# Weight loads move from SyncE's DMA queue to ScalarE's, and a padding write moves behind the first loads

## The chip, the cores and the metric

One NeuronCore of a Trainium2 chip runs the whole program. The metric is device time in microseconds (us), from the run's own time measurement; the profiler adds one profiled execution, whose span is counted from its first to its last instruction. The engines are named as in the profile: PE (matrix multiply), PEld (its weight loads), DVE (VectorE), ACT (ScalarE), POOL (GpSimd) and SP (SyncE). SP computes nothing here; it issues transfers. ACT and POOL can issue transfers too, as instructions in their own streams. A "q" behind an engine's name in the profile (SPq, ACTq) means its sequencer, which issues transfers and waits on semaphores, in order.

## The reference

```python
# 1. a gated linear scan over time, per batch and channel (4 x 5056 tokens, 256 channels)
sig = 1.0 / (1.0 + np.exp(-f_logit))
f = lower_bound + (1.0 - lower_bound) * sig
i = 1.0 - f
for t in range(S):
    h = f[:, t] * h + i[:, t] * x[:, t]
    y[:, t] = h
# 2. a mixture of 8 experts over the 20224 tokens of y, one expert per token
e_idx = np.argmax(y @ w_gate, axis=1)
gate_w = softmax(y @ w_gate)[token, e_idx]
eom = 1.0 / (1.0 + np.exp(-(y @ w_output_gate)))
for e in range(8):
    h = np.maximum(y[e_idx == e] @ w1[e], 0.0)          # 256 -> 1024
    out[e_idx == e] = gate_w * eom[:, e] * (h @ w2[e])  # 1024 -> 256
```

## The kernel before

The tokens are taken in 40 chunks of 512. For a chunk, `load_chunk` (lines 241 to 252) brings f and x, 512 KB each; below they are called f0 and x0 for chunk 0, f1 and x1 for chunk 1, and so on. `chunk` (line 254) then runs Tanh on ACT (line 265), a product on DVE (269), an affine step on ACT (274), the scan on DVE (280), a Square with a sum on ACT (287), a split of the result into a high and a low float16 part (310 on ACT, 314 on DVE), a transpose of these by DMA from SP (307), the gate logits and the choice of an expert (329 to 430), and last the scatter of the token rows from POOL into a scratch array in DRAM, sorted by expert (433). `scr` is that array; its last 128 rows are padding rows for tiles that have nothing to do, written once from the tile `padt` (lines 208 to 212).

An expert's tile of tokens is fetched from `scr` with two SP transfers, a transposing gather and its small metadata (`gather`, lines 624 to 638), goes through two matrix products, a scaling on ACT and a scatter from POOL into the output (754). There are two kinds of tiles. The "first" tiles (`first1`, `first2`, lines 712 to 741; 16 of them, 128 tokens each) run early, while the weights are still being prepared. The main tiles (`gemm1`, `gemm2`, lines 666 to 709) run in the long stage that begins at about 187 us.

The weights come as float32 and are turned into scaled float16 high and low parts. There are 16 halves (w1 and w2 of eight experts). `prep_load(j)` (lines 562 to 568) brings half j in two 512 KB pieces into the tile pool `wp`, which has 8 buffers, so four halves are there at a time. `prep_gram` and `prep_sum` (570, 590) find the scale on PE, `prep_hi` (612) writes the high part on ACT (line 614), `prep_lo` (616) the low part on DVE (line 619). Once the low part is written, the two buffers are free for half j + 4.

The order: lines 877 to 882 load chunks 0, 1 and 2 and halves 0 to 3, in the source order chunk 0, chunk 1, half 0, chunk 2, halves 1 to 3. The loop from line 884 on goes through the halves. At step j it issues `prep_load` for half j + 3 (line 886), runs pieces of the chunks and of the scaling, and feeds first tiles in between. `ordered` (lines 915 to 923) fixes what may be rearranged: up to the end of this early stage the instructions on DVE, ACT, PE and POOL are free, and the scheduler orders them by when they can run; SP's transfers keep the order of the source throughout, and behind the early stage everything does.

Of the kernel before, what the change touches and what calls it, by code (L numbers as in the profile page):

```python
# [45 lines left out]
def raw(ins):  # L46
    return getattr(ins, "ins", ins)
# [3 lines left out]
def tile_scan_moe(  # L51
# [10 lines left out]
    nc = tc.nc  # L62
    P = 128
# [10 lines left out]
    FREE = E * R  # L74
# [3 lines left out]
    WH = WE // 2  # L78
    QH = WH // 2
# [4 lines left out]
    def sure(tokens):  # L84
# [10 lines left out]
    scr = dp.tile([E * R + P, RW], I16, name="scr")  # L95
# [8 lines left out]
        out=tri, in_=ones, compare_op=ALU.is_gt, fill=0.0, base=0, pattern=[[1, P]], channel_multiplier=-1  # L104
# [63 lines left out]
    def alone(g):  # L168
# [12 lines left out]
        out=gsq, in0=wgf, scalar=1.0, in1=wgf, op0=ALU.mult, op1=ALU.mult, accum_out=gss  # L181
# [9 lines left out]
        out=wgs[:, :, 1, :], in0=wgc, scalar=gsc, in1=wgs[:, :, 0, :], op0=ALU.mult, op1=ALU.subtract  # L191
# [3 lines left out]
    fresh = []  # L195

    def apart(ins, group, keep=()):
        tc.declare_no_dep(raw(ins), group=group, keep=[raw(k) for k in keep], reason="rows apart")
        tc.add_to_no_dep_group(group, raw(ins))
# [8 lines left out]
    padt = cp.tile([P, RW], I16, name="padt")  # L208
    nc.gpsimd.memset(padt, 0)
    nc.gpsimd.iota(padt[:, CM + 2 : CM + 4].bitcast(I32), pattern=[[0, 1]], base=N, channel_multiplier=0)  # L210
    fresh.append(nc.sync.dma_start(out=scr[FREE : FREE + P, :], in_=padt))
    apart(fresh[0], "scr")
    row2 = [cp.tile([P, NB, RW], I16, name=f"rows{i}") for i in range(2)]

    top1 = w1f[:, (E - 1) * 2 * WH : E * 2 * WH]
# [346 lines left out]
    def prep_load(j):  # L562
        ws = []
        for i in range(2):
            w = wp.tile([P, QH], F32, tag="w", name="w")
            nc.sync.dma_start(out=w, in_=wT[j // 2][:, j % 2 * WH + i * QH : j % 2 * WH + (i + 1) * QH])
            ws.append(w)
        half[j] = dict(w=ws)

    def prep_gram(j):  # L570
        H = half[j]
        H["pg"] = pg = pp.tile([P, P], F32, tag="h", name="pg", bufs=4)
        nq = QH // P
        for i in range(2):
            rr = H["w"][i].bitcast(BF16).rearrange("p (c two) -> p c two", two=2)[:, :, 1]
            for q in range(nq):
                part = rr[:, q * P : (q + 1) * P]
                nc.tensor.matmul(out=pg, lhsT=part, rhs=part, start=(i + q == 0), stop=(i == 1 and q == nq - 1))

    def prep_norm(j):  # L580
        H = half[j]
        l2 = sp.tile([P, 1], BF16, tag="l2", name="l2")
        yield BIG
        jk = sp.tile([P, P], F16, tag="jk", name="jk", bufs=1)
        nc.vector.scalar_tensor_tensor(
            out=jk, in0=H["pg"], scalar=1.0, in1=ident, op0=ALU.mult, op1=ALU.mult, accum_out=l2
        )
        H["l2"] = l2

    def prep_sum(j):  # L590
        half[j]["pb"] = pb = pp.tile([P, 1], F32, tag="rw", name="pb")
        nc.tensor.matmul(out=pb, lhsT=ones, rhs=half[j]["l2"], start=True, stop=True)

    def prep_scale(j):
        H = half[j]
        H["sc"], H["iv"] = yield from pow2(H["pb"], TW, "w")
        if j % 2:
            e = j // 2
            yield SMALL
            nc.vector.scalar_tensor_tensor(  # L600
                out=cinv[:, e : e + 1], in0=half[j - 1]["iv"], scalar=0.125, in1=H["iv"], op0=ALU.mult, op1=ALU.mult
            )
# [9 lines left out]
    def prep_hi(j, z):  # L612
        h, r = parts(j, 0, z)
        nc.scalar.activation(h, r, AF.Copy, scale=half[j]["sc"])

    def prep_lo(j, z):
        (h, r), (l, _) = parts(j, 0, z), parts(j, 1, z)
        yield BIG
        nc.vector.scalar_tensor_tensor(out=l, in0=r, scalar=half[j]["sc"], in1=h, op0=ALU.mult, op1=ALU.subtract)
# [190 lines left out]
    def step(k, tasks, need=PLAN):  # L810
        prog["left"] += k
        if prog["left"] < 1.0:
            together(tasks)
        while prog["left"] >= 1.0:
            prog["left"] -= 1.0
            pump(tasks, need)
            tasks = []
# [17 lines left out]
    def early(j):  # L835

        if not line or line[0]["half"] == 1 and len(line) == 1:
            for r in range(len(firsts)):
                e = turns[r]
                if e < min(E, (j + 1) // 2) and (r == 0 or e < turns[r - 1]):  # L840
                    T = gather(f"f{r * E + e}", firsts[r][e], e)
                    T["half"] = 0
                    line.append(T)
                    turns[r] += 1
                    break
        tasks, wait, ready, late = [], list(pend), list(over), list(mid)
        pend.clear()
        over.clear()
        mid.clear()
        for T, h in wait:  # L850
            tasks.append(first_low(T, h))
            if h == 0:
                tasks.append(factors(T))
        go = line and line[0]["ev"] < j // 2

        def rest():
            for T in ready:
                evacuate(T)
                put(T)
            if go:  # L860
                T, h = line[0], line[0]["half"]
                T["half"] += 1
                if h == 1:
                    line.pop(0)
                first1(T, h)
                pend.append((T, h))
            for T, h in late:
                first2(T, h)
                if h == 1:
                    over.append(T)  # L870
            mid.extend(wait)

        return tasks, rest
# [3 lines left out]
    for n in range(min(EARLY[0], NCH)):  # L877
        load_chunk(n)
        if n:
            prep_load(n - 1)  # L880
    for n in range(min(EARLY[0], NCH) - 1, deep):
        prep_load(n)
    for j in range(-2, nh):
        tasks = []
        if 1 <= j < nh + 1 - deep:
            prep_load(j - 1 + deep)
        if 0 <= j + 1 < nh:
            tasks.append(prep_scale(j + 1))
        for z in range(2):
            if 0 <= j:  # L890
                tasks.append(prep_lo(j, z))
            mine, rest = early(j)
            tasks += mine
            step((PUMPS if j >= TURN else PUMPS0 if j >= 0 else FILL) / 2, tasks, LEAD)
            if 0 <= j + 1 < nh:
                prep_hi(j + 1, z)
            rest()
            tasks = []
            if j + 2 < nh:
                if z == 0:  # L900
                    prep_gram(j + 2)
                    tasks.append(prep_norm(j + 2))
                else:
                    prep_sum(j + 2)
# [110 lines left out]
```

## Time and profile before

| what | value |
|---|---|
| median of 3 runs | 1020.92 us (1020.44 to 1021.68) |
| the profiled execution's own time | 1019.5 us |
| its span | 1017.8 us |
| busy PE / PEld / DVE / ACT / POOL | 917.6 / 822.5 / 886.5 / 511.8 / 378.2 us |
| weight loads (line 566) | 32 of 512 KB, all on SP |
| chunk loads (lines 250, 251) | 80, all on SP |
| other transfers of ACT's queue | 2 (lines 122 and 123) |

How to read it: a line of the timeline gives the start, the time, the engine, the line of the kernel, the operation with its output and input, and how many of them the row merges; in brackets stands how long the engine was idle before, and what ended the idle time. A line of the waits gives who waited, for whom, the total in us, how often, and the longest. For a transfer, the row of SPq or ACTq is the issue, not the transfer itself; when it lands is seen at the instruction that waited for it.

### The profile page before, as it was taken

What the parts mean: (1) busy time and instruction counts of PE and PEld (TensorE: products, weight loads), DVE (VectorE), ACT (ScalarE), POOL (GpSimd) and SP (SyncE); (2) the same over time, 40 slices, a digit from 0 to 9 for tenths busy, and PEclk for the clock granted to TensorE, in tenths of its full rate; (3) what the DMA queues carried; (4) which work ended last, traced back from release to release, by engine and by line L of the source; (5) the groups of instructions that cost most, each with busy time, mean ns of one, the idle gap of its engine ahead of it and who ended that gap; (6) DMA issues with size and microseconds to landing.
All of it is one profiled execution on the core that took longest, in us unless ns stands there. A gap on an engine that the chain in (4) does not pass through costs nothing. (4 is left out here: it accounts for less than half of the span.)

```text
span 1017.8 us, 27499 instructions
## 1 busy us (share of the span) xinstructions
PE 917.6 (90%) x9775; PEld 822.5 (81%) x9775; DVE 886.5 (87%) x2803; ACT 511.8 (50%) x1075; POOL 378.2 (37%) x378
## 2 busy tenths in 40 slices
PE   2267998899999999999999999999999999999993
PEld 2156987788888888888888888888888888899993
DVE  7889897899999999999999999999999998758771
ACT  5667684554554555545545455455455543333331
POOL 1532334334344443433444434344444344221121
PEclk9999999999999999999999999999999999999997
DMA  8899976755655556456566555565565644321120
GB/s 311 200 305 271 254 179 147 163 154 137 139 136 151 145 136 163 135 136 142 132 141 156 157 147 133 136 139 132 142 154 135 151 91 97 97 54 43 43 55 16
DMA packets 238546, 146.34 MB, mean 144 GB/s; under 512 B 202557, under 2 KB 204223, under 8 KB 238400
## 3 DMA queue, kind: packets, MB, share of 16 engines
q1 hardware_dynamic: 222752, 101.74, 43.5%
q0 software_dynamic: 15360, 42.74, 13.3%
q8 instruction: 80, 1.31, 0.6%
q14 instruction: 66, 0.54, 0.2%
q10 hardware_dynamic: 288, 0.02, 0.0%
HBM read 58.38 MB, written 44.49 MB: 101 GB/s over the span
## 5 line engine op out<-in xcount | busy, mean ns | idle before, releaser
L675 PE MATMUL ph<-xq,w 128*128 128x256 f16 (+1 forms) x1312 | 331.0, 261 | 3.2 <-DMA xq<-scr 2.7
L677 PE MATMUL ph<-xq,w 128*128 128x256 f16 (+1 forms) x1312 | 331.6, 261 | 0.0
L676 PE MATMUL ph<-xq,w 128*128 128x256 f16 (+1 forms) x1312 | 331.3, 261 | 0.0
L706 PE MATMUL py<-w,hh 128*128 128x256 f16 x1168 | 318.0, 272 | 10.4 <-DVE w L663 5.5
L708 PE MATMUL py<-w,hl 128*128 128x256 f16 x1168 | 318.3, 273 | 0.0
L707 PE MATMUL py<-w,hh 128*128 128x256 f16 x1168 | 318.2, 272 | 0.0
L754 POOL DMA_INDIRECT out_dram<-yo,mt x146 | 165.9, 1137 | 298.4 <-ACT yo L750 270.5
L433 POOL DMA_INDIRECT scr<-rows,dst x154 | 178.9, 1162 | 225.3 <-issue 212.5
L680 ACT ACTIVATE hh<-ph 128x512 f16<-128x512 f32 (+1 forms) x328 | 178.7, 545 | 156.9 <-PE ph L677 154.9
L688 DVE SCALAR_TENSOR_TENSOR hl<-ph,hh 128x512 f16<-128x512 f32 (+1 forms) x328 | 204.8, 625 | 10.4 <-ACT hh L680 8.6
L675 PEld LDWEIGHTS <-w 128*128 128x128 f16 x1312 | 128.0, 98 | 16.5 <-DVE xt L269 3.0
L677 PEld LDWEIGHTS <-w 128*128 128x128 f16 x1312 | 128.1, 98 | 12.1
L657 DVE COPY w<-w1s 128x2048 f16 x164 | 114.9, 701 | 26.2 <-PE ph L677 24.7
L676 PEld LDWEIGHTS <-w 128*128 128x128 f16 x1312 | 127.9, 97 | 9.7
L707 PEld LDWEIGHTS <-hh 128*128 128x128 f16 x1168 | 113.9, 98 | 23.2 <-issue 12.7
L708 PEld LDWEIGHTS <-hl 128*128 128x128 f16 x1168 | 113.9, 98 | 13.5
L706 PEld LDWEIGHTS <-hh 128*128 128x128 f16 x1168 | 113.9, 98 | 11.2
L663 DVE COPY w<-w2s 128x2048 f16 x164 | 111.9, 682 | 0.5 <-PE py L708 0.3
L274 ACT ACTIVATE ft<-ft,fb,fa 128x512 f32<-128x512 f32 (+1 forms) x76 | 60.6, 807 | 97.9 <-DVE xt L269 90.1
L310 ACT ACTIVATE ft<-xt,sa 128x512 f16<-128x512 f32 (+1 forms) x76 | 50.2, 708 | 104.9 <-DVE li L299 100.7
L280 DVE TENSOR_TENSOR_SCAN xt<-ft,xt 128x512 f32<-128x512 f32 (+4 forms) x78 | 90.9, 1173 | 0.0
L750 ACT ACTIVATE yo<-py,fac 128x256 f32<-128x256 f32 x146 | 61.5, 465 | 26.4 <-PE py L708 22.8
(172 smaller groups left out, 1355.0 us busy)
## 6 DMA issues: line engine op xcount, KB each, us to landing
ft<-in_fT_dram SPq DMA_DIRECT2D x37, 512.0 KB
xt<-in_xT_dram SPq DMA_DIRECT2D x37, 512.0 KB
w<-in_wT_dram SPq DMA_DIRECT2D x32, 512.0 KB
scr<-rows,dst POOLq DMA_INDIRECT x154, 2.8
rows<-ft SPq DMA_TRANSPOSE x152
out_dram<-yo,mt POOLq DMA_INDIRECT x146, 2.4
xq<-scr SPq DMA_TRANSPOSE x99
scr<-padt SPq DMA_DIRECT2D x9, 136.0 KB
```

The lines of the kernel that those rows point to most:

```text
L433: ins = nc.gpsimd.indirect_dma_start(out=scr[:, :], out_offset=IOA(ap=dst[:, b : b + 1], axis=0), in_=rows[:, b, :], in_offset=None)
L657: nc.vector.tensor_copy(out=w, in_=w1f[:, ds(T["ev"] * (2 * WH) + h * 2 * QH, 2 * QH)])
L663: nc.vector.tensor_copy(out=w, in_=w2f[:, ds(T["ev"] * (2 * WH) + h * 2 * QH, 2 * QH)])
L675: nc.tensor.matmul(out=o, lhsT=w[:, f, k, 0, :], rhs=T["xh"][:, k, 0:n], start=first, stop=False)
L676: nc.tensor.matmul(out=o, lhsT=w[:, f, k, 0, :], rhs=T["xl"][:, k, 0:n], start=False, stop=False)
L677: nc.tensor.matmul(out=o, lhsT=w[:, f, k, 1, :], rhs=T["xh"][:, k, 0:n], start=False, stop=last)
L680: nc.scalar.activation(hh[:, :, 0:n], ph[:, :, 0:n], AF.Relu)
L688: nc.vector.scalar_tensor_tensor(out=hl[:, :, 0:n], in0=ph[:, :, 0:n], scalar=0.0, in1=hh[:, :, 0:n], op0=ALU.max, op1=ALU.subtract)
L706: nc.tensor.matmul(out=o, lhsT=hh[:, i, c], rhs=w[:, f, 0, :], start=first, stop=False, skip_group_check=True)
L707: nc.tensor.matmul(out=o, lhsT=hh[:, i, c], rhs=w[:, f, 1, :], start=False, stop=False, skip_group_check=True)
L708: nc.tensor.matmul(out=o, lhsT=hl[:, i, c], rhs=w[:, f, 0, :], start=False, stop=last, skip_group_check=True)
L754: ins = nc.gpsimd.indirect_dma_start(out=out[:, :], out_offset=IOA(ap=T["mt"][:, b, 2:4].bitcast(I32), axis=0), in_=T["yo"][:, b, :], in_o ...
```

## The change

The loads of the weights, 32 in all, are issued by ACT instead of SP. The write of the padding rows, SP's first transfer so far, is issued behind the loads of chunks 0, 1 and 2 (and stands in the source behind the first eight weight loads). Sizes, buffers and everything else stay.

```diff
     nc.gpsimd.iota(padt[:, CM + 2 : CM + 4].bitcast(I32), pattern=[[0, 1]], base=N, channel_multiplier=0)
-    fresh.append(nc.sync.dma_start(out=scr[FREE : FREE + P, :], in_=padt))
-    apart(fresh[0], "scr")
     row2 = [cp.tile([P, NB, RW], I16, name=f"rows{i}") for i in range(2)]
...
             w = wp.tile([P, QH], F32, tag="w", name="w")
-            nc.sync.dma_start(out=w, in_=wT[j // 2][:, j % 2 * WH + i * QH : j % 2 * WH + (i + 1) * QH])
+            nc.scalar.dma_start(out=w, in_=wT[j // 2][:, j % 2 * WH + i * QH : j % 2 * WH + (i + 1) * QH])
             ws.append(w)
...
     for n in range(min(EARLY[0], NCH) - 1, deep):
         prep_load(n)
+    fresh.append(nc.sync.dma_start(out=scr[FREE : FREE + P, :], in_=padt))
+    apart(fresh[0], "scr")
     for j in range(-2, nh):
```

## The prediction

> **What bounds the kernel now.** I read the page first, then the busy time by stage, then the timeline of the first 20 us, then the waits of SyncE's own queue.
>
> ```profile
> span 1017.8 us, 27499 instructions
> ```
>
> ```profile
> 0.00:52.40 52.40, 13.05 (x157) 10.47 (x157) 42.73 (x165) 32.63 (x64) 16.64 (x34) 1.00 0.87 252
> 52.40:126.60 74.20, 57.02 (x792) 53.42 (x793) 63.94 (x220) 49.93 (x85) 22.22 (x21) 0.98 1.06 278
> 126.60:187.00 60.40, 53.85 (x725) 49.41 (x723) 50.08 (x173) 37.30 (x72) 24.12 (x25) 0.97 0.67 158
> 187.00:900.00 713.00, 692.72 (x6762) 613.98 (x6760) 653.69 (x2086) 354.38 (x762) 292.02 (x277) 1.00 0.56 137
> ```
>
> The columns are busy us of PE, PEld, DVE, ACT and POOL, then PE clock, DMA share and GB/s. From 187 us on PE is busy 692.72 of 713 us (97%), so the long stage is PE-bound and the change touches none of its instructions: all weights have been loaded by 126 us. What the change is worth is decided before 187 us, and a shift there reaches the end nearly unshrunk, because the long stage has no idle time in which to catch up. In the first stage PE is idle and DVE is the busiest engine (42.73 of 52.4 us); it cannot begin chunk 0 before the chunk is there and ScalarE has taken its Tanh. So I look at who holds that start.
>
> ```profile
> 0.83 0.38 ACTq L122 DMA_DIRECT2D lbt<-in_lbT_dram  x1
> 1.23 0.45 ACTq L123 DMA_DIRECT2D wgc<-in_wgT_dram  x1
> 1.71 1.28 ACT L265 ACT_TABLE_LOAD   x1 [1.71 <-PEq L1004]
> 3.00 0.13 POOL L210 IOTA padt<- 128x1 int32 x1
> 3.16 0.38 SPq L211 DMA_DIRECT2D scr<-padt  x1
> 3.60 0.42 SPq L250 DMA_DIRECT2D w2s<-in_fT_dram  x1
> 7.66 0.63 ACT L265 ACTIVATE w2s<-w2s 128x512 f32<-128x512 f32 x1 [4.67 <-DMA w2s<-in_fT_dram]
> 7.88 0.47 SPq L566 DMA_DIRECT2D w<-in_wT_dram  x1
> 8.94 0.34 SPq L566 DMA_DIRECT2D w<-in_wT_dram  x1
> 9.06 0.69 DVE L269 SCALAR_TENSOR_TENSOR w2s<-w2s 128x512 f32<-128x512 f32 x1 [3.68 <-DMA w2s<-in_xT_dram]
> 14.01 0.33 SPq L566 DMA_DIRECT2D w<-in_wT_dram  x1
> 19.42 5.30 SPq L307 DMA_TRANSPOSE w1s<-w2s  x4
> ```
>
> ```profile
> SPq L211 <- POOL rows L398: 2.7, 1, 2.7
> SPq L566 <- DMA w<-in_wT_dram: 1.9, 2, 1.0
> SPq L566 <- DMA xt<-in_xT_dram: 0.9, 1, 0.9
> SPq L566 <- DMA ft<-in_fT_dram: 0.9, 1, 0.9
> SPq L566 <- DMA w2s<-in_xT_dram: 0.6, 1, 0.6
> ```
>
> Two things stand here. First, SyncE waits 2.7 us for POOL because its first instruction is the padding write, whose tile POOL finishes at 3.13 us; only then, at 3.60, the first load of chunk 0 goes out. Second, the last five weight loads, from 8.94 to 14.01 us, do not go out when the queue reaches them. Each waits for an earlier transfer, and the view names which: x of chunk 0, then f and x of chunk 1, then the first two weight pieces. Counted in order of issue (lbt, wgc, padding, f0, x0, f1, x1, two weights, f2, x2, six weights), these are the 13th to 17th transfers waiting for the 5th to 9th: a load issued by either queue waits until the one eight places ahead has landed. The five are (14.01 - 8.94) / 4 = 1.27 us apart, the time in which one 512 KB load drains. Today these waits cost little: they hold only SyncE, which has nothing ready to issue before 19.42 us anyway.
>
> **The padding write.** It goes behind the six chunk loads. SyncE then begins when nothing holds it; the nearest row is ScalarE's first load at 0.83 us, so f0 goes out 3.60 - 0.83 = 2.77 us sooner. The write's 0.38 us of issue lies where SyncE is empty (before 19.42). The first reader is a gather:
>
> ```profile
> 56.06 1.21 SPq L630 DMA_TRANSPOSE xq<-scr  x1
> 100.89 0.23 PE L719 MATMUL ph<-xq,w1s 128*128 128x128 f16 x1 [3.14 <-DMA xq<-scr]
> ```
>
> That is some 40 us of cover; without it the price would be one such wait for a gather, 3.14 us at most. I take nothing.
>
> **The first eight weight loads.** They move to ScalarE's queue, where they stand in the source (lines 877 to 882) ahead of everything that ScalarE computes. In the early stage the order of ScalarE's instructions is left to the scheduler (line 920), so their place is my assumption: they need nothing that is late, and an instruction that can go is placed before a Tanh that still waits for data. Then ScalarE's queue reads lbt, wgc, eight weight loads, table load, Tanh, and the waits seen above now hold ScalarE. The last weight load is the 16th or 17th transfer (the padding behind or before it), so it waits for the 8th or 9th. lbt and wgc are two of those, so that is the sixth or seventh large load. In the trace x0, the second large one, had landed by 8.94, which is 5.34 us after f0's issue, and the sixth by 14.01, 10.41 us after it. With f0 issued at 0.83, the sixth lands at 0.83 + 10.41 = 11.24, the seventh at 12.51. On ScalarE follow 0.33 of issue, 1.28 of table load and 0.63 for the first Tanh: DVE starts at 13.48 to 14.75 instead of 9.06, which is 4.4 to 5.7 us late. If the table load were placed ahead of the loads (its row bears line 265, the Tanh's, yet it ran directly behind the second load, so the trace does not decide), it is 3.1 to 4.4. By then all of chunk 1 is there, so nothing else is late next; DVE, busy without a long gap from 9.06 on today, carries the delay along, and behind it the transposes of line 307. I take +5.0, the middle of the case with the table load. The row gives the table load 1.28 us. The Trainium skill, "ScalarE: Activation LUTs", section "What ACT_TABLE_LOAD costs", agrees on that figure but adds a drain of about 1.38 us to each switch of set; by it the sum would be 6.4, an estimate, and no row of this trace shows the drain.
>
> **The other 24 weight loads.** They are issued between 52.6 and 126 us.
>
> ```profile
> L566 SPq DMA_DIRECT2D w<-in_wT_dram x24: 328/392/1102, 52.6 to 125.7; - x24
> ```
>
> ```profile
> SPq L566 <- DVE w1s L619: 3.3, 2, 2.0
> SPq L566 <- DVE fc L424: 2.2, 2, 1.9
> PE ph L719 <- DMA xq<-scr: 9.7, 6, 3.1
> DVE xt L269 <- DMA xt<-in_xT_dram: 1.8, 1, 1.8
> DVE el L730 <- ACT eh L723: 2.1, 2, 1.5
> ```
>
> What SyncE gains: its gathers and chunk loads no longer stand behind weight loads. PE waited 9.7 us for gathers in this stage, so that is the ceiling; but a gather gains only where a weight load held it last.
>
> ```profile
> 69.95 4.97 SPq L566 DMA_DIRECT2D w<-in_wT_dram  x4
> 75.67 1.27 SPq L630 DMA_TRANSPOSE xq<-scr  x1
> 82.88 0.22 PE L719 MATMUL ph<-xq,w1s 128*128 128x128 f16 x1 [0.15 <-DMA xq<-scr]
> 81.51 1.02 SPq L566 DMA_DIRECT2D w<-in_wT_dram  x2
> 85.58 1.22 SPq L630 DMA_TRANSPOSE xq<-scr  x1
> 90.04 0.22 PE L719 MATMUL ph<-xq,w1s 128*128 128x128 f16 x1 [1.27 <-DMA xq<-scr]
> 96.13 1.04 SPq L566 DMA_DIRECT2D w<-in_wT_dram  x2
> 97.96 1.24 SPq L630 DMA_TRANSPOSE xq<-scr  x1
> ```
>
> The longest block, 4.97 us before the gather at 75.67, cost PE 0.15 us. The gather at 85.58 came 3 us after the weights, so they did not hold it. The one at 97.96 followed weights directly and PE waited 3.14 us at 100.89; 1.04 of that is theirs. DVE's 1.8 us for an x load is also partly theirs. Bounds 0 and 9.7; I take -1.5, near the rows that show a weight load directly ahead.
>
> What ScalarE pays: 24 x 0.392 = 9.4 us of issue, and the waits for DVE to free a buffer (5.5 us in the two largest groups), behind which Relu, Tanh and the weight scaling now queue. ScalarE has 74.2 - 49.9 = 24.3 us idle here, so most of it fits; who would feel the rest is DVE, which waits only 2.1 us for ScalarE's Relu today. Bounds 0 and 9.4 (less than 0 has no ground: ScalarE loses no work); I take +1.5, near the row in which DVE waits for ScalarE.
>
> **The sum.** +5.0 - 1.5 + 1.5 = +5.0 us. The profiled execution took 1019.5 us (span 1017.8) and would take 1024.5. The median of the runs shown, 1020.92, lies 1.4 above it, so the forecast for the median is 1025.9.
>
> **Rivals.** *Faster:* the weight loads are placed behind the first Tanh, or ScalarE is not held by the landings. Then only the earlier f0 counts. x0 had landed by 8.94, 5.34 after f0's issue, so it could land at 6.17; if two weight loads drain ahead of it from the other queue, at 8.71. DVE starts 0.35 to 2.9 us sooner, say 1.6; with -1.5 for SyncE and 0.5 for ScalarE, whose loads then sit in its gaps, that is -2.6: 1018.3 us. Against it speaks the source order, and that SyncE was held by just these waits; for it, that the order on ScalarE is free. It decides from the point at which the first Tanh starts before 7.66 us. *No difference:* the table load goes first (+3.1), SyncE gets back 3.5 of PE's 9.7 us, ScalarE's part is 0.5: +0.1, 1021.0 us. The Trainium skill, "DMA: Bandwidth & Descriptors", section "Issuing engines are not separate DMA queues", speaks for this one: transfers of all issuing engines run on the same 16 DMA engines, and a second issuer saves only the usually small issue time. The stage 52 to 126 us, with a DMA share of 1.06, agrees; the rule says nothing of the ScalarE work behind a held issue. *Worse:* the start costs 5.0 and half of the 9.4 us of issue falls on DVE's path, with nothing gained on SyncE: +9.7, 1030.6 us. DVE's 86% busy time in that stage speaks for it, ScalarE's 24 us of idle time against.
>
> **How the numbers follow.** Forecast 0.54, worse 0.07, faster 0.22, no difference 0.17. A measurement of this kernel can tell about 0.2%, 2 us, from no change. Slower by more than that: 0.54 + 0.07 = 0.61; within 0.17; faster 0.22. The forecast's own range is 1023.2 to 1029 (start 3.1 to 5.7, the other terms moving by 1 to 2); to hold 8 in 10 it must reach most of the faster case and the edge of the worse one: 1017.5 to 1031.
>
> **What would show it.** Right: SyncE's first load at about 0.8 us; ten loads on ScalarE's queue ahead of its first Tanh, the last ones 1.27 us apart; Tanh at 12 to 14 us; DVE's line 269 at 13 to 15; the first L680 some 5 us later than today, and PE from there to the end as busy as before. Wrong: a Tanh at 5 to 6 us with weight loads behind it; a start that is late but made up by 187 us, through gathers that come sooner; or a late start that grows, with DVE waiting for ScalarE in the 52 to 126 us stage.

## The result and the profile after

| kernel | median | runs | ratio to before |
|---|---|---|---|
| before | 1020.68 us (1020.25 to 1021.68) | 4 | 1 |
| changed | 1060.88 us (1053.95 to 1066.89) | 4 | 1.039, 95% interval 1.0326 to 1.0454 |

The change makes the kernel 40.2 us slower: slower as forecast, but eight times as much as the +5.0 us of the sum. The profiled execution of the changed kernel took 1061.26 us, its span is 1059.6 us. Lines behind 212 are lower by two in it (Tanh is line 263, DVE's product 267, the weight loads 564).

First the busy time by stage, with the columns of the table shown of before:

```profile
0.00:52.40 52.40, 13.12 (x155) 10.27 (x156) 35.60 (x150) 26.73 (x54) 6.76 (x25) 1.00 0.78 236
52.40:126.60 74.20, 35.82 (x437) 32.77 (x437) 54.44 (x182) 41.94 (x69) 22.25 (x23) 0.90 0.85 231
126.60:187.00 60.40, 49.48 (x701) 46.40 (x700) 43.01 (x132) 35.23 (x61) 15.43 (x16) 0.96 0.64 151
187.00:900.00 713.00, 681.21 (x6759) 602.81 (x6758) 649.32 (x2091) 358.80 (x777) 296.01 (x282) 1.00 0.57 139
```

Against before, PE does 21.2 us less in the second stage (57.02 to 35.82), 4.4 less in the third and 11.5 less between 187 and 900 us; that work comes at the end. The first Relu of the long stage (line 680, now 678) starts at 229.3 us instead of 187.0, 42.3 us late, and the whole span is 41.8 us longer. So the loss arises ahead of the long stage, as predicted, but most of it not at the start. POOL, which scatters the rows, does 6.76 us in the first stage instead of 16.64.

The timeline of the first 20 us, SP's and ACT's queues with the first instructions behind them:

```profile
0.83 0.45 SPq L248 DMA_DIRECT2D w2s<-in_fT_dram  x1
1.76 14.81 ACTq L564 DMA_DIRECT2D w<-in_wT_dram  x8
3.38 0.37 SPq L248 DMA_DIRECT2D ft<-in_fT_dram  x1
16.60 1.28 ACT L263 ACT_TABLE_LOAD   x1 [16.60 <-DMA ft<-in_fT_dram]
17.89 1.15 ACT L263 ACTIVATE w2s<-w2s 128x512 f32<-128x512 f32 x2
18.55 1.29 DVE L267 SCALAR_TENSOR_TENSOR w2s<-w2s 128x512 f32<-128x512 f32 x2 [11.86 <-ACT w2s L263]
```

And one line of the chain of waits (start, us, what):

```profile
3.38 12.83 DMA ft<-in_fT_dram
```

The eight weight loads do stand ahead of the first Tanh, and the last of them waits for the transfer eight places before it, f2: the brackets of the table load, ACT's next instruction, name it. f2 went out at 3.38 and landed 12.83 us later, at 16.21. DVE starts at 18.55 instead of 9.06: 9.5 us late, where 4.4 to 5.7 was expected.

The delay then does not stay the same. The Tanh of chunks 0, 2, 5, 7 and 9 is at 7.66, 17.65, 56.67, 99.01 and 148.29 us before, and at 17.89, 22.81, 72.40, 121.76 and 180.08 after: 10.2, 5.2, 15.7, 22.8 and 31.8 us late. Chunk 2 has caught up half; chunk 9 has lost three times the start. The first scatter, the first gather and the longest wait for a gather on PE:

```profile
47.28 1.14 POOL L431 DMA_INDIRECT scr<-w1s,dst  x1 [43.88 <-DVE es L417]
70.32 1.27 SPq L628 DMA_TRANSPOSE xq<-scr  x1
78.91 0.27 PE L717 MATMUL ph<-xq,w1s 128*128 128x128 f16 x1 [12.45 <-DMA xq<-scr]
```

The scatter is 13.4 us late (33.91 before), the gather 14.3. The waits in the second stage (who, for whom, total us, times, longest):

```profile
PE ph L717 <- DMA xq<-scr: 20.4, 2, 12.5
PE pv L289 <- ACT ft L285: 8.7, 2, 7.6
DVE fac L647 <- DMA mt<-scr: 7.3, 2, 4.5
ACT ft L285 <- DVE xt L278: 4.7, 3, 3.5
DVE el L728 <- ACT eh L721: 2.1, 1, 2.1
```

DVE waits for ACT's Relu as long as before (2.1 us); the prediction had named a growth of this wait as the sign of a late start that grows. PE waits for gathers 20.4 us instead of 9.7, and 8.7 us for ACT's Square (line 285), for which it did not wait before; that Square in turn waits 4.7 us for DVE's scan. So the largest growth here is that of the gathers, which come late.

### The profile page after: what moved, and what is told of

Same layout as the page of the kernel before. It is cut to its first block, busy times and chain, and to the rows that moved or that the text cites. A ratio compares the mean times of both kernels' runs of the same rounds, so it can differ in the third digit from the quotient of the medians.

```text
span 1059.6 us, 27479 instructions
## 1 busy us (share of the span) xinstructions
PE 922.1 (87%) x9775; PEld 824.7 (78%) x9775; DVE 887.8 (84%) x2803; ACT 513.1 (48%) x1075; POOL 374.2 (35%) x378
## 4 chain that ended last, share of the span: by engine, by line
DVE 53%; issue 17%; DMA 13%; PE 9%; POOL 3%; ACT 2%; DVEq 1%; POOLq 0%; ACTq 0%; SPq 0%
DVE hl L686 11%; DVE xt L278 7%; DVE w L655 5%; DMA rows<-ft 4%; DVE w L661 4%; DVE xt L267 4%; DVE ft L312 2%; POOL out_dram L752 2%; DMA xq<-scr 2%; DMA scr<-rows,dst 2%; DMA ft<-in_fT_dram 2%; DMA out_dram<-ey,mt 1%; PE ph L673 1%; PE ph L674 1%; PE ph L675 1%
## 5 line engine op out<-in xcount | busy, mean ns | idle before, releaser
L704 PE MATMUL py<-w,hh 128*128 128x256 f16 x1168 | 317.7, 272 | 11.5 <-DVE w L661 5.9
L431 POOL DMA_INDIRECT scr<-rows,dst x154 | 175.7, 1141 | 257.5 <-issue 228.9
L673 PEld LDWEIGHTS <-w 128*128 128x128 f16 x1312 | 128.3, 98 | 15.7 <-DVE w L655 2.7
L285 ACT ACTIVATE ft<-xt 128x512 f32<-128x512 f32 (+1 forms) x76 | 48.0, 631 | 56.6 <-DVE xt L278 53.4
```

The costliest lines, as they stand in the source:

```text
L431: ins = nc.gpsimd.indirect_dma_start(out=scr[:, :], out_offset=IOA(ap=dst[:, b : b + 1], axis=0), in_=rows[:, b, :], in_offset=None)
L673: nc.tensor.matmul(out=o, lhsT=w[:, f, k, 0, :], rhs=T["xh"][:, k, 0:n], start=first, stop=False)
L704: nc.tensor.matmul(out=o, lhsT=hh[:, i, c], rhs=w[:, f, 0, :], start=first, stop=False, skip_group_check=True)
```

## The experiments

Theory A: ACT is held, by the issues of the weight loads and the waits in front of them. Theory B: in the early stage the scheduler places the instructions of PE, DVE, ACT and POOL anew, and the new order costs. The two kernels' instruction lists speak for B: of DVE's 530 computing instructions of this stage 492 stand at another place than before, of PE's 1652 1049, though the diff touches none of them. All ratios are to the kernel before, run beside on the same chip, with 95% intervals; a difference of two ratios is given in us of 1020.

**The parts alone, order left free.** `e1_pad` moves only the padding write; `e2_w` moves only the weight loads; `e3_first8` has the padding moved and the first eight weight loads on ACT, `e4_last24` the other 24.

The edit of `e3_first8` against the changed kernel:

```diff
-            nc.scalar.dma_start(out=w, in_=wT[j // 2][:, j % 2 * WH + i * QH : j % 2 * WH + (i + 1) * QH])
+            (nc.scalar if j < 4 else nc.sync).dma_start(out=w, in_=wT[j // 2][:, j % 2 * WH + i * QH : j % 2 * WH + (i + 1) * QH])
```

In `e4_last24` the two queues are exchanged in that line; `e1_pad` and `e2_w` are the hunks of the change by themselves.

> Only the padding write is moved; all weight loads stay on SyncE. Theory A (ScalarE is held: its weight loads wait in its queue for earlier transfers, and all it computes queues behind them) and theory B (the scheduler's new order of the engines' instructions does not fit the times on the chip) both expect no cost here: f0 goes out at about 0.8 us, DVE's line 269 starts at 6 to 7 us instead of 9.06, so 0 to 3 us faster than before, 1018 to 1021 us. A time above 1025 would make the padding write part of the loss.

> Only the weight loads move to ScalarE; the padding write stays first on SyncE. Theory A: chunk 0's first load goes out at 3.6 us again and the eight loads hold ScalarE as before, so the whole loss is here, 1055 to 1065 us. If the loss needed both edits (chunk loads and weight loads starting in the same microsecond), it would be below 1045.

> The padding write is moved and only the first eight weight loads go to ScalarE, the other 24 stay on SyncE. Theory A in its simple form (each held load costs where it stands): the start is 9 to 10 us late as in the changed kernel and nothing is added later, 1029 to 1033 us. Theory B: the order made for an early start does not fit the late one, and the delay grows without any held load, 1045 to 1060 us.

> The padding write is moved, the first eight weight loads stay on SyncE, the other 24 go to ScalarE. Theory A: the rest of the loss, 40 less 10, stands here: 1040 to 1052 us, with ScalarE's issues waiting and DVE or PE idle behind them between 50 and 150 us. Theory B: the start fits the order again, so little is lost, 1018 to 1030 us.

| run | ratio | interval |
|---|---|---|
| e1_pad | 1.0072 | 1.0051 to 1.0092 |
| e2_w | 1.0381 | 1.0328 to 1.0434 |
| e3_first8 | 1.0213 | 1.0162 to 1.0264 |
| e4_last24 | 1.0245 | 1.0177 to 1.0314 |

Moving the weight loads is the loss; each of its two parts alone costs over 2% (at least 1.6% by the intervals). Between the theories these runs do not decide: `e2_w` came out as theory A said, `e4_last24` (about 1045 us for a kernel of 1020) within A's range and far from B's, `e3_first8` (about 1042 us) between the two. Both theories missed `e1_pad`: chunk 0's Tanh comes 3.0 us sooner (4.64), and yet the kernel is 0.7% slower. Nothing holds ACT there, so theory A has no ground for it; a new order has, and so would the padding write itself. The next runs therefore fix the order.

**The order fixed.** A list of places is written into the kernel, and every computing instruction of the early stage on PE, DVE, ACT and POOL is tied behind the one that stands ahead of it in that list. ACT's loads keep the freedom and SP's transfers the order that they had. `e5_hold` is the changed kernel in the order of before; `e6_order` has the weights on SP, the padding moved, and the order of the changed kernel; `e7_pad_pin` is `e1_pad` and `e8_late_pin` is `e4_last24`, both in the order of before.

```diff
+        for eng in (nc.tensor, nc.vector, nc.scalar, nc.gpsimd):
+            n = a.pop(0)
+            line, a = a[:n], a[n:]
+            mine = [
+                i for i in nc.cur_bb.bb.instructions[:cut]
+                if i.engine == eng.engine and not (eng is nc.scalar and type(i).__name__ == "InstDMACopy")
+            ]
...
+            for p, q in zip(line[:-1], line[1:]):
+                tc.add_manual_dep(mine[q], mine[p].name, AFTER, reason="pinned")
```

> The changed kernel, with every computing instruction of TensorE, VectorE, ScalarE and GpSimd in the first stage tied to the order that it had in the kernel before; the 32 weight loads are on ScalarE's queue, the first eight ahead of its first Tanh, and the padding write is behind the first loads. Theory A (ScalarE's loads and their waits hold the chain): nearly the whole loss stays, ratio 1.035 to 1.045. Theory B (the changed kernel loses because the scheduler gave its instructions another order): only the late start is left, about 9.5 us, ratio 1.005 to 1.012. In between: both, and the share is read from this run.

> Weight loads on SyncE's queue as before, padding write behind the first loads, and every computing instruction of the first stage tied to the order that the changed kernel has. Theory A: nothing holds ScalarE, so it stands with the run in which the padding write alone moved, ratio 1.00 to 1.01. Theory B: the order alone costs 20 to 30 us, ratio 1.02 to 1.03.

> Padding write behind the first loads, weight loads on SyncE's queue, computing order of the first stage tied to that of the kernel before. Where the padding write alone moved, with the order free, the ratio was 1.0072. Theory B (that loss was the new order): it goes, and the earlier start shows, 0 to 2 us faster, ratio 0.997 to 1.001. Theory A (the padding write itself does harm where it now stands): ratio 1.005 to 1.009 again.

> As the run with padding write moved and the 24 later weight loads on ScalarE's queue (ratio 1.0245 with the order free), with the computing order of the first stage tied to that of the kernel before. Theory A (the waits of the 24 issues on ScalarE hold its activations): the loss stays, 1.02 to 1.03. Theory B (the order): 0.998 to 1.005, that is, the 24 issues cost at most 5 us.

| what stands where | order free | order of before |
|---|---|---|
| padding moved | 1.0072 (1.0051 to 1.0092) | e7: 0.9982 (0.9964 to 1.0000) |
| and 24 loads on ACT | 1.0245 (1.0177 to 1.0314) | e8: 1.0087 (1.0054 to 1.0120) |
| and all 32 on ACT (the change) | 1.0390 (1.0326 to 1.0454) | e5: 1.0233 (1.0202 to 1.0265) |

`e6_order`, nothing on ACT but the order of the change: 1.0203 (1.0171 to 1.0235). Both theories hold a part, and neither is the whole. The order alone costs 23 us (1.0203 against 0.9982), or 16 us of the change (1.0390 against 1.0233); the move alone 26 us (1.0233 against 0.9982). Together they are 42 (1.0390 against 0.9982), less than the sum. Tying the instructions costs nothing that can be told, as `e7_pad_pin` is level with the kernel before. And the loss of `e1_pad` was order: with that of before it is gone. `e8_late_pin` lies between the ranges of the two theories.

What the order does is seen in the timelines of DVE, POOL and PE. With the order of before (`e7_pad_pin`):

```profile
17.65 1.41 DVE L360 SCALAR_TENSOR_TENSOR w2s<-w2s,sa 128x512 f16<-128x512 f32 x2
20.30 2.45 DVE L326 TENSOR_TENSOR_SCAN xt<-ft,xt 128x512 f32<-128x512 f32 x2
30.17 0.23 DVE L476 TENSOR_SCALAR w1s<-fc,xi 128x4 f32<-128x4 f32 x1
31.32 1.47 POOL L479 DMA_INDIRECT scr<-w1s,dst  x1 [27.91 <-DVE w1s L315]
58.57 0.27 PE L765 MATMUL ph<-xq,w1s 128*128 128x128 f16 x1 [2.45 <-DMA xq<-scr]
```

With the order of the change (`e6_order`):

```profile
19.28 1.27 DVE L325 TENSOR_TENSOR_SCAN xt<-ft,xt 128x512 f32<-128x512 f32 x1
20.52 1.27 DVE L325 TENSOR_TENSOR_SCAN xt<-ft,xt 128x512 f32<-128x512 f32 x1
21.76 0.74 DVE L359 SCALAR_TENSOR_TENSOR w2s<-w2s,sa 128x512 f16<-128x512 f32 x1
22.48 0.74 DVE L359 SCALAR_TENSOR_TENSOR w2s<-w2s,sa 128x512 f16<-128x512 f32 x1
37.15 0.22 DVE L475 TENSOR_SCALAR w1s<-fc,xi 128x4 f32<-128x4 f32 x1
38.30 1.14 POOL L478 DMA_INDIRECT scr<-w1s,dst  x1 [34.87 <-DVE og L420]
66.76 0.27 PE L764 MATMUL ph<-xq,w1s 128*128 128x128 f16 x1 [9.46 <-DMA xq<-scr]
```

Chunk 0 lies in the tile w2s. In the old order DVE splits it (17.65) and then takes the scans of a later chunk; in the new order it takes those scans first and splits chunk 0 at 21.76. The metadata of chunk 0's rows is ready at 37.15 instead of 30.17, and the first scatter goes out 7.0 us later, though the first Tanh starts just as early (4.62 us, 4.57 in the old order). PE's first product on a gathered tile starts 8.2 us later, after a wait of 9.5 us instead of 2.5.

**What the move costs with the order fixed.** In `e8_late_pin` the first divergence from `e7_pad_pin` is at chunk 5. The timeline of `e7_pad_pin`:

```profile
48.91 0.52 SPq L296 DMA_DIRECT2D ft<-in_fT_dram  x1
54.05 1.15 ACT L311 ACTIVATE ft<-ft 128x512 f32<-128x512 f32 x2 [0.85 <-DMA ft<-in_fT_dram]
```

and of `e8_late_pin`:

```profile
45.49 0.36 ACTq L612 DMA_DIRECT2D w<-in_wT_dram  x1
46.75 0.35 ACTq L612 DMA_DIRECT2D w<-in_wT_dram  x1
49.12 0.91 SPq L296 DMA_DIRECT2D ft<-in_fT_dram  x1
52.95 0.34 ACTq L612 DMA_DIRECT2D w<-in_wT_dram  x1
57.31 0.63 ACT L311 ACTIVATE ft<-ft 128x512 f32<-128x512 f32 x1 [3.89 <-DMA ft<-in_fT_dram]
60.91 0.69 DVE L315 SCALAR_TENSOR_TENSOR xt<-ft,xt 128x512 f32<-128x512 f32 x1 [4.99 <-DMA xt<-in_xT_dram]
```

f5 goes out at the same time, but needs 8.2 us until its Tanh instead of 5.1, and DVE waits 5.0 us for x5. ACT is not held by its issues there; it waits for data itself. On SP's queue those weight loads went out behind x5. Over the whole second stage the gathers are late too. The waits of `e7_pad_pin`, for gathers and for their small metadata:

```profile
PE ph L765 <- DMA xq<-scr: 6.6, 4, 2.4
DVE fac L695 <- DMA mt<-scr: 3.1, 4, 1.6
```

and of `e8_late_pin`:

```profile
PE ph L765 <- DMA xq<-scr: 14.8, 3, 8.3
DVE fac L695 <- DMA mt<-scr: 8.5, 2, 7.3
```

This makes theory C: the weight loads, on a queue of their own, run beside transfers that are awaited. `e9_behind_f` places each of the 24 in ACT's stream behind the Tanh of the chunk whose f and x went ahead of it on SP in `e7_pad_pin`; `e10_behind_tanh` is `e5_hold` with the first eight behind the Tanhs of chunks 0 and 1; `e11_both` does both. (Load k goes behind chunk c's Tanh, by so many computing instructions of ACT as `later` says, 0 to 12, so that the loads of one chunk don't go out all at once.)

```diff
+        for k, (c, later) in BEHIND.items():
+            at = mine[acts[spot[tanh[2 * c + 1].name] + later]]
+            tc.add_manual_dep(load[k - FIRST], at.name, AFTER, reason="behind")
```

> As the run with the 24 later weight loads on ScalarE's queue and the computing order of before (ratio 1.0087), but each of the 24 is placed in ScalarE's line behind the Tanh of that chunk whose f and x SyncE issued ahead of the same load when it stood on SyncE's queue. So no weight load goes out beside the f that the next Tanh waits for. Theory C (the 24 cost because on a queue of their own they run beside f and x and take their share of the transfers; there, f of the sixth chunk took 8.2 us from issue to Tanh instead of 5.1 and DVE waited 5.0 us for its x): most of the loss goes, 0.998 to 1.003. Theory A (the issues and waits on ScalarE cost): it stays, 1.007 to 1.012.

> The changed kernel with the computing order of before (ratio 1.0233), but of the first eight weight loads four stand behind the first chunk's Tanh on ScalarE and four behind the second chunk's, none ahead of the first. Theory A (the first eight hold the first Tanh by 10 us or more, and the rest of the 15 us between this kernel and the one with the first eight on SyncE is that start carried on): the first Tanh is back at 4 to 5 us and the ratio falls to 1.007 to 1.013. If the eight cost by being on another queue at all: 1.018 to 1.024 stays.

> All 32 weight loads on ScalarE's queue and the padding write behind the first loads, as in the changed kernel; computing order of before; the first eight behind the Tanhs of the first two chunks and the 24 behind the Tanhs of the chunks whose f and x go first. If the three causes (other order, held first Tanh, transfers beside f and x) are the whole loss, it is gone: ratio 0.997 to 1.004, beside 0.998 for the same order with the loads on SyncE. If the queue itself costs something that is none of the three: 1.01 or more.

| run | ratio | interval |
|---|---|---|
| e9_behind_f | 1.0132 | 1.0109 to 1.0155 |
| e10_behind_tanh | 1.0141 | 1.0118 to 1.0164 |
| e11_both | 1.0149 | 1.0109 to 1.0190 |

`e10_behind_tanh` gains 9.4 us on `e5_hold` (1.0141 against 1.0233), a little less than theory A said: its first Tanh is back at 4.48 us. So the held start is worth 9.4 us, give or take 4. ACT is not quite free in it. Behind the first Tanh it still waits for landings, where the weight loads stand in its stream:

```profile
8.34 1.52 ACT L324 ACTIVATE w2s<-w2s,fb,fa 128x512 f32<-128x512 f32 x2 [2.72 <-DMA ft<-in_fT_dram]
13.87 0.63 ACT L337 ACTIVATE w2s<-w2s 128x512 f32<-128x512 f32 x1 [2.97 <-DMA w<-in_wT_dram]
```

`e9_behind_f` and `e11_both` missed: theory C in this narrow form falls. The timeline of `e9_behind_f` shows where the time goes at first:

```profile
53.77 1.13 ACT L315 ACTIVATE ft<-ft 128x512 f32<-128x512 f32 x2
59.70 0.83 ACTq L616 DMA_DIRECT2D w<-in_wT_dram  x2
62.48 1.07 ACTq L616 DMA_DIRECT2D w<-in_wT_dram  x2
75.39 0.39 SPq L300 DMA_DIRECT2D ft<-in_fT_dram  x1
80.02 0.63 ACT L315 ACTIVATE ft<-ft 128x512 f32<-128x512 f32 x1 [6.55 <-DMA ft<-in_fT_dram]
```

Chunk 5's Tanh is back (53.77), but now the weights run beside SP's row transposes and gathers (57 to 65 us). f6 goes out at 75.39, where it went at 67.64 in `e7_pad_pin`. It waits for a row transpose that was issued at 61.39 and took 13.92 us to land, by the chain of waits. From 30 to 190 us these waits of SP's f loads are

```profile
SPq L300 <- DMA rows<-ft: 14.7, 3, 5.1
```

where `e7_pad_pin` has 3.8 us from 8 to 230 us. The collision was moved, not removed. Left are two readings: the 512 KB transfers on the second queue, or the issues on ACT after all. `e12_small` is `e7_pad_pin`, all weights on SP, with 24 tiny loads at the places of `e9_behind_f`:

```diff
             nc.sync.dma_start(out=w, in_=wT[j // 2][:, j % 2 * WH + i * QH : j % 2 * WH + (i + 1) * QH])
+            if j >= 4:
+                k = len(small)
+                small.append(nc.scalar.dma_start(out=bits[:, k : k + 1], in_=lbT[:, 0:1]))
```

> The kernel with only the padding write moved and the computing order of before (all 32 weight loads on SyncE's queue, ratio 0.9982), and beside them 24 more loads on ScalarE's queue, each of one 4-byte element per partition, at the places in ScalarE's line where the run before last had the 24 weight loads (ratio 1.0132 there). The extra loads are read by nothing. They cost ScalarE's issues and take their turns in the wait for the eighth transfer before, but move no bytes to speak of. Theory A (issues and waits on ScalarE, and the shared turns, cost 10 us or more): 1.006 to 1.014. Theory C, widened (what costs is the 512 KB transfers running on a second queue beside f, x, the transposes and the gathers): 0.997 to 1.002.

Measured: 0.9991 (0.9978 to 1.0004). The issues on ACT, and their turns among the eight, cost 0.9 us against `e7_pad_pin`, give or take 2.3; so what costs comes with the large transfers. (The tiny loads wait for no weight buffer. But neither did ACT in `e8_late_pin`: the 22 semaphore instructions ahead of its weight loads took 17 ns each.) The view of the DMA traffic from 40 to 130 us (q1 is SP's queue, q10 ACT's; packets, MB, share of the 16 engines' time). `e7_pad_pin`:

```profile
DMA packets 21893, 23.99 MB, mean 267 GB/s; under 512 B 15840, under 2 KB 15840, under 8 KB 21881
q1 hardware_dynamic: 20585, 20.13, 82.7%
```

`e8_late_pin`:

```profile
DMA packets 19844, 19.70 MB, mean 219 GB/s; under 512 B 15008, under 2 KB 15008, under 8 KB 19833
q10 hardware_dynamic: 2592, 9.44, 42.2%
q1 hardware_dynamic: 16041, 6.68, 38.0%
```

`e12_small`:

```profile
DMA packets 25057, 23.99 MB, mean 267 GB/s; under 512 B 19008, under 2 KB 19008, under 8 KB 25045
q1 hardware_dynamic: 20581, 20.11, 86.4%
q10 hardware_dynamic: 3168, 0.01, 4.6%
```

With the weights on ACT's queue the same 90 us move 19.70 MB instead of 23.99. This is no proof that the engines moved less than they could: the 9.44 MB of q10 are 18 loads of 512 KB, where `e7_pad_pin` moves all 24 in this time. Two of the other six had gone out before it, at 26.5 and 28.1 us, and four come too late for it. They make 3.1 of the missing 4.3 MB. With tiny loads on ACT's queue the figure stays at 23.99 MB.

## Why the prediction was wrong

**What held.** The eight loads ahead of the first Tanh, the wait for the transfer eight places before, the loss ahead of the long stage and its way to the end undiminished: all as predicted. The sign is right, and for the reason given (the held start alone costs 9.4 us), but three quarters of the loss came in ways for which the sum has no term or one of the wrong sign.

**The start, +5.0: mis-sized, 9.5 at DVE.** The step that failed is "With f0 issued at 0.83, the sixth lands at 0.83 + 10.41 = 11.24, the seventh at 12.51." It took the order of landing from the order of issue on one queue. f2, the load that was waited for, is the fifth large one on SP's queue, and it landed at 16.21. Weight loads on ACT's queue drained beside it: in the first 17 us the two queues moved 3.20 and 2.64 MB. At the step's own spacing of 1.27 us, 16.21 is 2.9 places behind 12.51, the place of the tenth load and not of the seventh. In time, `e5_hold` against `e10_behind_tanh` puts the held start at 9.4 us.

**"DVE ... carries the delay along": failed.** The prediction let all else follow at one distance. The scheduler's freedom (the order on DVE, ACT, PE and POOL is left free up to the end of the early stage) was read only for the place of the eight loads on ACT. But with it 492 of DVE's 530 instructions change their place: 16 us of the change, give or take 7, and 23 alone. This is the largest term, and the sum has none for it.

**The other 24 loads, -1.5 and +1.5: the first failed, the second is not refuted.** ACT's price is 0.9 us, give or take 2.3 (`e12_small` against `e7_pad_pin`: 0.9991 and 0.9982). SP's relief is a loss: `e8_late_pin` against `e7_pad_pin` is +10.7 us, outside the bounds of 0 and 9.7 that allowed a gain only. The bound was taken from gathers that stand behind a weight load on SP. That weights on a second queue would make awaited transfers late had no row in the trace of before, where the large loads stood on one queue, and the term should have been bounded on the other side as well. The DMA share of 1.06 in that stage, quoted for the rival without a difference, could have warned of it. The Trainium skill, "DMA: Bandwidth & Descriptors", section "Issuing engines are not separate DMA queues", says that transfers of all issuers interleave on the same 16 engines; the runs agree, and f5's 8.2 us instead of 5.1 fits it. But that a second issuer does no more than save the issue time, as the prediction took from the same section, did not hold here: +10.7 us.

**The padding write, 0: right for what it does**, with the order held (0.9982, 1.8 us faster with an upper end of 1.0000, for a start 3.1 us sooner). Alone and with the order free it costs 0.7%, again by the order.

The parts with the order of before, each from two ratios: padding -1.8, the 24 loads +10.7, the first eight behind the Tanhs +5.5 (1.0141 against 1.0087), held start +9.4, order +16.0. That they add up to the change is no check, as each run is the start of the next difference. By the intervals each is good to 2 to 7 us, and they depend on what else is in place (the order alone costs 23). The rivals failed too: "worse" reached +9.7 and named ACT's issues, of which no cost can be told.

**What stays open.** Within the price of the large transfers, the share of the engines and the waits for the eighth transfer before, which can grow when those transfers slow down, were not separated; that holds for the 24 and for the 5.5 us of the first eight. Nor was another place for the 24 found that costs nothing: `e9_behind_f` is 4.6 us above `e8_late_pin`, give or take 4, and in it PE also waited 6.0 us for weights themselves. Why the scheduler's new order is worse was seen for chunk 0's routing only.

No version clearly beats the kernel before: `e7_pad_pin` is at the edge of what can be told.

## What to carry to other kernels

A single queue that always has work also keeps an order: here the awaited loads went first and the weights behind them. On a second queue the weights ran beside them. Before such a move, ask for each awaited transfer what will now share its time, and how late it may land. Where a scheduler orders the computing, a change of a queue changes that order too: fix the order first (as `e7_pad_pin` does), measure the change, and only then read the sum.

## What the hardware showed that was not expected

A 512 KB load with four such loads ahead of it on its own queue took 12.83 us to land while eight more stood on the other queue. And 24 loads of 128 four-byte elements each took 4.6% of the DMA engines' time from 40 to 130 us for 0.01 MB, without a measurable cost to the kernel.
